# Front products of the second MoE: another order of seven products, copies by ScalarE for additions by VectorE, and another end

## The chip, the cores and the metric

The kernel runs on one core of one Trainium2 chip. TensorE multiplies, VectorE, ScalarE and GpSimd work elementwise, SyncE issues the transfers. The metric is the device time of one execution in microseconds. A matmul is fp32 split in two fp32r parts ("hi" and "lo"): three matmuls (hi x hi, hi x lo, lo x hi) add up in a PSUM bank, which only TensorE, VectorE and ScalarE can reach.

## The reference, cut to what matters

```python
x = attention(q, k, v, p)                 # 4 x 8 heads, 576 tokens, 32 packed queries
h = x @ w_in;  x = (h * cos(h)) @ w_out   # first MoE: 2304 tokens, 512 -> 2048 -> 512
p = domain_probs / (domain_probs.sum(-1, keepdims=True) + 1e-09)
for e in range(4):                        # second MoE: 512 -> 1024 -> 512 for each e
    h = np.maximum(x @ w1[e], 0.0)
    out += p[:, e:e + 1] * (h @ w2[e])
```

The change touches only the second MoE.

## The kernel before, in words

Attention and the first MoE fill the time up to about 395 us. The second MoE cuts the 2304 tokens into three thirds (h = 0, 1, 2) and w1 and w2 into eight units u of 512 hidden columns: 24 steps, n = 8h + u. Each step has a front (x @ w1) and a back (h @ w2); the back of step n stands beside the front of step n + 1.

**The front** uses a scheme with seven block products for the eight of a 2x2 block multiplication (names as in `PRODUCTS`, line 654: s1 to s4 are sums of blocks of w1, t1 to t4 of tokens). `b_pair` (line 926) makes one pair of halves, j = 0 or 1, so there are 48 pairs of seven products, each of six matmuls over 384 columns (`prod`, `mm3`). With P1 = a11 b11, P2 = a12 b21, P3 = s4 b22, P4 = a22 t4, P5 = s1 t1, P6 = s2 t2 and P7 = s3 t3: c11 = P1 + P2, u2 = P1 + P6, u3 = u2 + P7, c12 = u2 + P5 + P3, c21 = u3 - P4 (the sign lies in t4), c22 = u3 + P5. A pair holds two PSUM tiles `pa` of two banks each; there are four such tiles, and backs and fronts share them. ScalarE copies P1 into an SBUF tile `p` (line 1020); VectorE makes the five additions (line 958, three into `p`, two into a bank). Then `relu` splits each of the four blocks into hi and lo (first third; lines 1007 and 1010), or `gated` applies max(x, 0) and the token's share in one operation (line 975), and line 987 makes the sums that the back needs, lines 667 and 658 their hi and lo.

**The back** of the first third is plain (`b_back`, line 1050). For the other two thirds `b_back2` (line 1099) uses seven products again (`BACK`, line 1093), each 12 matmuls, in four tiles A to D. Each is added into one of the accumulators v, w, c11, x53, x74 by line 1132 (first time) or 1134. After the last unit of a third `final` adds x53 += v, w += x53 and x74 += v (line 1149), and `put` stores four blocks (line 1156).

**Operands.** In the first third w1 and w2 are loaded, summed, split and also stored in DRAM; in the other thirds they come back from there. The plain blocks of w2 come from a DRAM copy (`copy_w2`, line 1315, issued during the first MoE) and are split on arrival: ScalarE makes hi (`f_hi` in `split_in_place`, line 705), GpSimd or VectorE lo. Pools of this stage open at three gates; `pt`, which holds the tiles `p`, opens at gate 3 (line 1312), after the last operations of the first MoE are placed.

**The order** of all engines is made by a planner, `Plan` (line 27), and then written out as it stands (line 1375): each engine's queue is in order. It places operations one by one at the earliest time at which their inputs, buffers (`pl.slot`, with a count for each tag) and engine are free. TensorE's operations have keys (`KEYS`, by place in the step: `first`, `one`, `two`, `end` for fronts and backs, `last` for the last back); TensorE may take an operation only if its key is at most `AHEAD` = 60 above the smallest key that is left. Durations are constants of the source, times `pl.slow` in this stage. The entry `b` of `KEYS` has one key for each line of `BACK`; before, `last` has 357.6 for the fourth (w1, into x53) and 165.9 for the seventh (a22, into x74):

```python
if eng == "PE" and o["key"] > pe[0][0] + ahead:
    ok = False
...
'last': {'b': [39.4, 45.5, 37.7, 357.6, 51.2, 27.5, 165.9]},
```

Of the kernel before, what the change touches and what calls it, by code (L numbers as in the profile page):

```python
# [10 lines left out]
F32 = mybir.dt.float32  # L11
# [3 lines left out]
AF = mybir.ActivationFunctionType  # L15
ALU = mybir.AluOpType
# [10 lines left out]
class Plan:  # L27
# [35 lines left out]
    def run(self):  # L63
# [15 lines left out]
        while done < len(self.ops):  # L79
# [33 lines left out]
            t, _, o, eng = best  # L113
# [21 lines left out]
            for x, w in [(x, fin) for x in o["next"]] + [(x, t) for x in o["then"]]:  # L135
                x["wait"] -= 1
                x["at"] = max(x["at"], w)
                if not x["wait"]:
                    todo[x["eng"]].append(x)
# [7 lines left out]
def tile_packed_attention_moe_moe2(ctx: ExitStack, tc: tile.TileContext, qT, kT, vk, pT, w_in, w_out, dp, w1, w2, out, out2):  # L147
# [61 lines left out]
    def pool(name, side, bufs=1):  # L209
# [8 lines left out]
               "raw": 4, "s": 4, "aop": 8, "w2": 8, "ys": 5, "pt": -6, "g2": 13, "oacc": NTT,  # L218
# [5 lines left out]
    def dma(us, f, after=(), take=(), use=(), key=None, begun=()):  # L224
        return pl.op("SP", us, f, after, take, use, key, begun=begun)
# [700 lines left out]
    def b_pair(n, j, W, T, keys, share=None):  # L926
# [4 lines left out]
        sp = {"a": pl.slot("pa"), "c": pl.slot("pa")}  # L931
        sp["b"], sp["d"] = sp["a"], sp["c"]
        st_ = {x: pl.slot("pt") for x in ("p1", "u2", "u3")}

        def prod(i, bank, first, after):
            a, b = PRODUCTS[i]

            def f():
                if bank in "ac" and first:
                    x = psum2()  # L940
                    s[bank], s["bd"["ac".index(bank)]] = x[:, 0, :TB], x[:, 1, :TB]
# [4 lines left out]
            return pl.op("PE", 1.06, f, [W[a]["ready"], T[b]["ready"]] + after, [sp[bank]] if bank in "ac" and first else [],  # L946
                         [sp[bank], W[a]["slot"], T[b]["slot"]], keys[i])

        def tmp(name):
            s[name] = bp["pt"].tile([P, TB], F32, tag="p", name="p", bufs=6)  # L950
            return s[name]

        def add(o, x, y, after, key):
            new = o in st_ and o not in s_new
            s_new.add(o)

            def f():
                nc.vector.tensor_tensor(out=s[o] if o in s else tmp(o), in0=s[x], in1=s[y], op=ALU.add)  # L958
            return pl.op("DVE", 0.56, f, after, [st_[o]] if new else [], [sp[x], sp.get(o) or st_[o], st_[y]], key)
# [3 lines left out]
        def gated(x, half, src, after, key):  # L963
            if src in st_:
                U[x] = {"slot": st_[src]}
            else:
                U[x] = {"slot": pl.slot("s" if x == "b21" else "raw" if n == NU else "oacc")}

            def f():
                U[x]["t"] = o = s[src] if src in st_ else {  # L970
                    "b21": lambda: bp["stp"].tile([P, TB], F32, tag="s", name="u", bufs=4),
                    "raw": lambda: bp["raw"].tile([P, TB], F32, tag="raw", name="u", bufs=4),
                    "oacc": lambda: bp["oacc"].tile([P, TB], F32, tag="oacc", name="u", bufs=NTT),
                }[x if x == "b21" else "raw" if n == NU else "oacc"]()
# [3 lines left out]
            U[x]["op"] = pl.op("DVE", 0.56, f, [after, share["op"], last_out[0] if src not in st_ and x != "b21" and n == NU + 1 else None],  # L978
                               [] if src in st_ else [U[x]["slot"]],
                               [share["slot"], U[x]["slot"]] + ([sp[src]] if src in sp else []), key, port=src not in sp)  # L980
# [17 lines left out]
        def relu(f_, half, src, after, key):  # L998
# [4 lines left out]
            use = [sp[src]] if src in sp else [st_[src]]  # L1003
# [5 lines left out]
            def f_lo():  # L1009
# [4 lines left out]
            g["ready"] = pl.op("DVE", 0.56, f_lo, [h], [], [g["slot"]] + use, key, port=src not in sp)  # L1014
            return g["ready"]

        s_new = set()
# [81 lines left out]
    def b_back2(n, W, keys):  # L1099
# [4 lines left out]
        for i, (a, b, bank, new, acc, how) in enumerate(BACK):  # L1104
# [22 lines left out]
            def f_evac(ob=ob, ac=ac, acc=acc, how=how, first=first):  # L1127
                p = ob["t"][:, :, :TB]
                if first:
                    ac["t"] = (bp["ys"].tile([P, 2, TB], F32, tag="ys", name="acc", bufs=5) if acc == "x53" else  # L1130
                               bp["raw"].tile([P, 2, 512], F32, tag="raw", name="acc", bufs=4)[:, :, :TB])
                    nc.scalar.activation(ac["t"], p, AF.Copy, scale=-1.0 if how == ALU.subtract else 1.0)
                else:
                    nc.vector.tensor_tensor(out=ac["t"], in0=ac["t"] if how == ALU.subtract else p,  # L1134
                                            in1=p if how == ALU.subtract else ac["t"], op=how)

            m = pl.op("PE", 2.08, f_mm, [g["ready"] for g in gl] + [w["ready"] for w in ws] + ([] if new else [free[bank]]),
                      [ob["slot"]] if new else [], [ob["slot"]] + [g["slot"] for g in gl] + [w["slot"] for w in ws], keys[i])
            free[bank] = ac["op"] = pl.op("ACT" if first else "DVE", 0.85 if first else 0.96, f_evac, [m, ac["op"]],
                                          [ac["slot"]] if first else [], [ob["slot"], ac["slot"]], keys[i] + 8)  # L1140
            last[0] = m
        if u < NU - 1:
            return

        def final(x, y, key):
            a, b = accs[h, x], accs[h, y]

            def f():
                nc.vector.tensor_tensor(out=a["t"], in0=a["t"], in1=b["t"], op=ALU.add)

            a["op"] = pl.op("DVE", 0.95, f, [a["op"], b["op"]], [], [a["slot"], b["slot"]], key, port=True)

        def put(x, i, c, key):
            def f():
                t0 = (h - 1) * TH + c * TB
                nc.sync.dma_start(out=out2[i * 256:(i + 1) * 256, t0:t0 + TB].rearrange("(d p) n -> p d n", p=P),
                                  in_=accs[h, x]["t"])

            dma(0.4 * MB2, f, [accs[h, x]["op"]], [], [accs[h, x]["slot"]], key)
# [15 lines left out]
    def share_ops():  # L1175
# [10 lines left out]
        def f_store():  # L1186
# [11 lines left out]
            'copy': [715.7, 22.6],  # L1198
# [7 lines left out]
            'keep': [117.2, -167, 205.3, 42.6],  # L1206
            'kept': [173.4, 203.5],
            'last': {'b': [39.4, 45.5, 37.7, 357.6, 51.2, 27.5, 165.9]},
# [27 lines left out]
            'one': {'a': [7.9, 13.2, 18.6, 61.7, 42.4, 68.2, 50.5, 39, 15.5, 61.8, 75.1, 71.4, 76.6, 72.1],  # L1236
                    'b': [14.1, 54.6, 76.5, 77.4, 55.9, 66.8]},
            'out0': [-122.9, -853.4],
            'two': {'a': [-11.2, 43, 29.3, 19.8, 20.5, 46.9, 7.1, 23, 52.9, 69, 21.4, 71.4, 100.2, 84.8],
                    'b': [8, 40.1, 58.9, 16.6, 79.4, 52.2, 103.3]}}  # L1240
# [86 lines left out]
    pl.slow, pl.late = 1.04, 0.8  # L1327
# [11 lines left out]
    for n in range(NSTEP + 1):  # L1339
# [11 lines left out]
        for j in range(2):  # L1351
            b_pair(n, j, Ws[n], Ts[h], [k0 + x for x in place["a"][7 * j:7 * j + 7]], share if h else None)
# [65 lines left out]
```

## Time and profile before

| | |
|---|---|
| three timed runs | 1150.52, 1151.81, 1153.53 us; median 1151.81 |
| the profiled execution | 1149.58 us, its span 1147.8 us |
| TensorE busy | 1101.7 us (96%), 7241 matmuls |
| VectorE busy | 835.3 us (73%) |
| GpSimd busy | 633.2 us (55%) |
| ScalarE busy | 493.4 us (43%) |
| mean granted clock of TensorE | 0.987 |

PE is TensorE, PEld its loads of weights, DVE VectorE, ACT ScalarE, POOL GpSimd, SP SyncE; SPq is SyncE's sequencer, which issues transfers. L958 is line 958 of the kernel. All matmuls stand under lines 205 to 207 (`mm3`): `pa<-bop,aop` are front products, `pa<-g,w` are matmuls of the first MoE or of backs of the last two thirds, `pa<-w,g` and `pa<-at,m` others. Matmuls are pipelined and their ends are modelled. The releaser of a wait is inferred from semaphores.

### The profile page before, as it was taken

What the parts mean: (1) busy time and instruction counts of PE and PEld (TensorE: products, weight loads), DVE (VectorE), ACT (ScalarE), POOL (GpSimd) and SP (SyncE); (2) the same over time, 40 slices, a digit from 0 to 9 for tenths busy, and PEclk for the clock granted to TensorE, in tenths of its full rate; (3) what the DMA queues carried; (4) which work ended last, traced back from release to release, by engine and by line L of the source; (5) the groups of instructions that cost most, each with busy time, mean ns of one, the idle gap of its engine ahead of it and who ended that gap; (6) DMA issues with size and microseconds to landing.
All of it is one profiled execution on the core that took longest, in us unless ns stands there. A gap on an engine that the chain in (4) does not pass through costs nothing.

```text
span 1147.8 us, 19120 instructions
## 1 busy us (share of the span) xinstructions
PE 1101.7 (96%) x7241; PEld 1032.5 (90%) x7241; DVE 835.3 (73%) x1244; ACT 493.4 (43%) x852; POOL 633.2 (55%) x477
## 2 busy tenths in 40 slices
PE   6689999999999999999999999999999999999997
PEld 4568999999999988888888889999999999999997
DVE  3798777567555677787777756888887768778776
ACT  3677655445444453244334434333334343333331
POOL 1454755435422775555566546656667767645553
PEclk8699999999999999999999999999999999999999
DMA  9673436433135859787866967676667876666653
GB/s 314 231 263 118 161 116 266 188 130 141 43 105 188 280 196 325 265 301 256 291 257 263 335 259 249 232 252 233 244 227 249 306 265 238 226 227 219 228 182 110
DMA packets 96815, 257.70 MB, mean 225 GB/s; under 512 B 10892, under 2 KB 34516, under 8 KB 94548
## 3 DMA queue, kind: packets, MB, share of 16 engines
q1 hardware_dynamic: 96724, 256.48, 63.1%
q8 instruction: 57, 0.93, 0.3%
q14 instruction: 34, 0.28, 0.1%
HBM read 192.97 MB, written 71.86 MB: 231 GB/s over the span
## 4 chain that ended last, share of the span: by engine, by line
PE 78%; DVE 8%; DMA 5%; issue 4%; ACT 3%; POOL 2%; SPq 0%; POOLq 0%; ACTq 0%; DVEq 0%
PE pa L205 26%; PE pa L207 25%; PE pa L206 25%; DMA w<-w 3%; PE pa L353 2%; DVE pa L958 1%; DVE s L755 1%; POOL aop L658 1%; POOL w L658 1%; DMA kt<-kT 1%; DVE acc L1134 1%; DVE p L958 1%; DVE u L975 0%; DVE oacc L1077 0%; DVE g L1010 0%
## 5 line engine op out<-in xcount | busy, mean ns | idle before, releaser
L205 PE MATMUL pa<-g,w 128*128 128x288 f32 (+1 forms) x960 | 303.6, 316 | 2.0 <-DVE acc L1134 0.8
L206 PE MATMUL pa<-g,w 128*128 128x288 f32 (+1 forms) x960 | 301.6, 314 | 1.2 <-POOL g L590 1.2
L207 PE MATMUL pa<-g,w 128*128 128x288 f32 (+1 forms) x960 | 301.2, 314 | 0.5 <-POOL w L297 0.5
L658 POOL TENSOR_TENSOR g<-u,g 128x384 fp32r<-128x384 f32 x157 | 171.5, 1105 | 140.3 <-ACT g L667 133.5
L205 PE MATMUL pa<-bop,aop 128*128 128x384 f32 x672 | 228.8, 341 | 9.3 <-DVE p L958 4.1
L207 PE MATMUL pa<-bop,aop 128*128 128x384 f32 x672 | 226.9, 338 | 1.5 <-POOL aop L658 1.5
L206 PE MATMUL pa<-bop,aop 128*128 128x384 f32 x672 | 226.3, 337 | 1.1 <-POOL bop L658 1.1
L205 PEld LDWEIGHTS pa<-g,w 128*128 128x128 f32 x960 | 180.1, 188 | 7.9 <-issue 2.4
L206 PEld LDWEIGHTS pa<-g,w 128*128 128x128 f32 x960 | 180.2, 188 | 1.9 <-POOL g L590 1.9
L207 PEld LDWEIGHTS pa<-g,w 128*128 128x128 f32 x960 | 180.4, 188 | 1.0 <-POOL w L297 1.0
L667 ACT ACTIVATE g<-u 128x384 fp32r<-128x384 f32 x192 | 97.2, 523 | 176.8 <-DVE u L987 134.9
L590 POOL TENSOR_TENSOR g<-t,g 128x576 fp32r<-128x576 f32 x64 | 93.2, 1470 | 118.8 <-ACT g L587 117.4
L205 PEld LDWEIGHTS pa<-bop,aop 128*128 128x128 f32 x672 | 126.1, 188 | 19.1 <-DVE p L958 6.1
L206 PEld LDWEIGHTS pa<-bop,aop 128*128 128x128 f32 x672 | 126.2, 188 | 3.0 <-POOL bop L658 1.4
L207 PEld LDWEIGHTS pa<-bop,aop 128*128 128x128 f32 x672 | 126.1, 188 | 2.2 <-POOL aop L658 2.2
L958 DVE TENSOR_TENSOR p<-pa,p 128x384 f32<-128x384 f32 x144 | 79.3, 554 | 41.4 <-PE pa L207 38.7
L1134 DVE TENSOR_TENSOR acc<-pa,acc 128x768 f32<-128x768 f32 x88 | 83.9, 954 | 32.6 <-PE pa L207 31.3
L658 POOL TENSOR_TENSOR w<-w 128x512 fp32r<-128x512 f32 x62 | 86.3, 1403 | 31.4 <-ACT w L705 31.2
L205 PE MATMUL pa<-at,m 128*128 128x288 f32 x256 | 78.7, 307 | 3.1 <-DVE t L583 2.0
L206 PE MATMUL pa<-at,m 128*128 128x288 f32 x256 | 77.5, 303 | 2.8 <-POOL at L658 2.8
L205 PE MATMUL pa<-w,g 128*128 128x512 f32 x192 | 75.9, 395 | 1.9 <-DVE oacc L1077 1.9
L207 PE MATMUL pa<-at,m 128*128 128x288 f32 x256 | 77.2, 301 | 0.0
(129 smaller groups left out, 1924.8 us busy)
## 6 DMA issues: line engine op xcount, KB each, us to landing
at<-at SPq DMA_DIRECT2D x16, 1152.0 KB, 5.3
raw<-w SPq DMA_DIRECT2D x32, 512.0 KB, 5.2
w<-w SPq DMA_DIRECT2D x64, 256.0 KB, 5.0
raw<-w_in SPq DMA_DIRECT2D x6, 1024.0 KB, 6.1
raw<-w_out SPq DMA_DIRECT2D x6, 1024.0 KB, 8.0
vt<-vk SPq DMA_DIRECT2D x8, 576.0 KB, 8.5
kt<-kT SPq DMA_DIRECT2D x8, 576.0 KB, 10.5
qt<-qT SPq DMA_DIRECT2D x8, 576.0 KB, 8.6
```

What stands on the lines that cost most here:

```text
L205: nc.tensor.matmul(o, lhsT=l(0), rhs=r(0), start=first, stop=False, skip_group_check=True)
L206: nc.tensor.matmul(o, lhsT=l(0), rhs=r(1), start=False, stop=False, skip_group_check=True)
L207: nc.tensor.matmul(o, lhsT=l(1), rhs=r(0), start=False, stop=last, skip_group_check=True)
L353: nc.tensor.matmul(o(e)[32 * q:32 * q + 32, :N], lhsT=l[64 * e:64 * e + 64, 32 * q:32 * q + 32], rhs=r(q // 2, q % 2)[64 * e:64 * e + 64], ...
L590: nc.gpsimd.tensor_tensor(out=s["g"][:, 1], in0=s["t"], in1=s["g"][:, 0].bitcast(F32), op=ALU.subtract)
L658: (nc.vector if on_vector else nc.gpsimd).tensor_tensor(out=dst[:, 1], in0=src, in1=dst[:, 0].bitcast(F32), op=ALU.subtract)
L667: nc.scalar.activation(r["t"][:, 0], src(), AF.Copy)
L755: nc.vector.tensor_tensor(out=t, in0=src(a, m)(), in1=src(b, m)(), op=o)
L958: nc.vector.tensor_tensor(out=s[o] if o in s else tmp(o), in0=s[x], in1=s[y], op=ALU.add)
L1134: nc.vector.tensor_tensor(out=ac["t"], in0=ac["t"] if how == ALU.subtract else p, in1=p if how == ALU.subtract else ac["t"], op=how)
```

## The change

Within a pair the products run as P1, P2, P6, P5, P7, P3, P4 (their keys are sorted). P1, P6, P7 and P4 add up one after another in bank a, so that it holds P1, u2, u3 and c21 in turn; ScalarE copies it out after P1 (p1) and after P6 (u2). P2 stands in bank b, P5 and then P3 in bank d; ScalarE copies d after P5 (p5). VectorE adds b += p1 (c11), e = a + p5 (c22, written to a bank) and d += u2 (c12). P6 waits for the copy p1, P7 for the copy u2, P3 for the copy p5, P4 for the addition of c22. There are eight tiles `p` for six, and the gated c22 gets a tile of its own for its place.

In the last back of a third, `final` and `put` stand inside the loop: c11 is stored after i = 2; x74 += v, x53 += v and w += x53 are made, and x53 and w stored, after i = 5; the product with i = 6 is added into x74 in two halves, each stored by itself.

The planner no longer adds 0.25 us between a product and a product that follows from it, slows VectorE, ScalarE and GpSimd by 1.08 for 1.04, and has other keys for this stage and for the DRAM copies of w2.

```diff
-            for x, w in [(x, fin) for x in o["next"]] + [(x, t) for x in o["then"]]:
+            for x, w in [(x, t + us if o["fair"] and eng == "PE" == x["eng"] else fin) for x in o["next"]] + [(x, t) for x in o["then"]]:
...
-               "raw": 4, "s": 4, "aop": 8, "w2": 8, "ys": 5, "pt": -6, "g2": 13, "oacc": NTT,
+               "raw": 4, "s": 4, "aop": 8, "w2": 8, "ys": 5, "pt": -8, "g2": 13, "oacc": NTT,
...
+        def keep(x, bank, after, key):
+            return pl.op("ACT", 0.5, lambda: nc.scalar.activation(tmp(x), s[bank], AF.Copy), [after, gate[3]], [st_[x]],
+                         [sp[bank]], key)
...
-        P1 = prod(0, "a", True, [])
-        p1 = pl.op("ACT", 0.5, lambda: nc.scalar.activation(tmp("p1"), s["a"], AF.Copy), [P1, gate[3]], [st_["p1"]], [sp["a"]],
-                   k[0] + 6)
-        P6 = prod(1, "b", True, [P1])
-        u2 = add("u2", "b", "p1", [P6, p1], k[1] + 6)
-        P7 = prod(2, "c", True, [])
-        u3 = add("u3", "c", "u2", [P7, u2], k[2] + 6)
-        P5 = prod(3, "d", True, [P7])
-        c22 = add("u3", "d", "u3", [P5, u3], k[3] + 6)
-        r22 = relu(2 + j, 1, "u3", c22, k[3] + 30)
-        P2 = prod(4, "a", False, [p1])
-        relu(j, 0, "a", P2, k[4] + 8)
-        P4 = prod(5, "c", False, [u3])
-        c21 = add("c", "c", "u2", [P4], k[5] + 6)
-        relu(2 + j, 0, "c", c21, k[5] + 30)
-        P3 = prod(6, "d", False, [c22, c21])
-        c12 = add("d", "d", "u2", [P3, c21], k[6] + 6)
-        relu(j, 1, "d", c12, k[6] + 30)
+        P1 = prod(0, 0, "a", True, [])
+        p1 = keep("p1", "a", P1, k[0] + 6)
+        P2 = prod(4, 1, "b", True, [], [P1])
+        relu(j, 0, "b", add("b", "b", "p1", [P2, p1], k[1] + 6), k[1] + 30)
+        P6 = prod(1, 2, "a", False, [p1])
+        u2 = keep("u2", "a", P6, k[2] + 6)
+        P5 = prod(3, 3, "d", True, [])
+        P7 = prod(2, 4, "a", False, [u2])
+        p5 = keep("p5", "d", P5, k[3] + 6)
+        c22 = add("e", "a", "p5", [p5, P7], k[4] + 6)
+        relu(2 + j, 1, "e", c22, k[4] + 30)
+        P3 = prod(6, 5, "d", False, [p5])
+        relu(j, 1, "d", add("d", "d", "u2", [P3, u2], k[5] + 6), k[5] + 30)
+        P4 = prod(5, 6, "a", False, [c22])
+        relu(2 + j, 0, "a", P4, k[6] + 30)
...
+            if u == NU - 1 and i == 6:
+                for d in range(2):
+                    ac["op"] = pl.op("DVE", 0.56, lambda d=d, f=f_evac: f(slice(d, d + 1)), [m, ac["op"]], [],
+                                     [ob["slot"], ac["slot"]], keys[i] + 8)
+                    put(h, acc, 1, 0, keys[i] + 12, d)
+                continue
...
-        kf = keys[-1] + 20
-        put("c11", 0, 0, kf)
-        final("x53", "v", kf + 1), final("w", "x53", kf + 2), final("x74", "v", kf + 3)
-        put("x53", 0, 1, kf + 10), put("w", 1, 1, kf + 11), put("x74", 1, 0, kf + 12)
+            if u == NU - 1 and i == 2:
+                put(h, "c11", 0, 0, keys[i] + 20)
+            if u == NU - 1 and i == 5:
+                final(h, "x74", "v", keys[i] + 9), final(h, "x53", "v", keys[i] + 10)
+                put(h, "x53", 0, 1, keys[i] + 20)
+                final(h, "w", "x53", keys[i] + 11)
+                put(h, "w", 1, 1, keys[i] + 21)
...
-            'copy': [715.7, 22.6],
+            'copy': [828.4, 90],
...
-            'last': {'b': [39.4, 45.5, 37.7, 357.6, 51.2, 27.5, 165.9]},
+            'last': {'b': [23.7, 34.9, 61.9, 308.4, 80.1, 226.3, 229]},
...
-    pl.slow, pl.late = 1.04, 0.8
+    pl.slow, pl.late = 1.08, 0.8
...
-            b_pair(n, j, Ws[n], Ts[h], [k0 + x for x in place["a"][7 * j:7 * j + 7]], share if h else None)
+            b_pair(n, j, Ws[n], Ts[h], [k0 + x for x in sorted(place["a"][7 * j:7 * j + 7])], share if h else None)
```

The other entries of `KEYS` for this stage change too (`end`, `first`, `g`, `keep`, `kept`, `one`, `two`).

## Rows read from the trace of the kernel before

**Rows 1.** The page's engine line, and the view of the cores.
```profile
PE 1101.7 (96%) x7241; PEld 1032.5 (90%) x7241; DVE 835.3 (73%) x1244; ACT 493.4 (43%) x852; POOL 633.2 (55%) x477
...
core 0: 1147.8 us, clock 0.987
```

**Rows 2.** Windows: stretch, its length, busy us of each engine, clock, DMA.
```profile
395.00:692.00 297.00, 287.17 (x1436) 255.80 (x1435) 217.02 (x323) 121.52 (x233) 173.96 (x121) 1.00 0.76 274
692.00:1148.00 456.00, 443.38 (x2512) 437.34 (x2510) 355.00 (x525) 160.73 (x308) 274.53 (x235) 1.00 0.66 231
```

**Rows 3.** Waits of TensorE, whole span: waiter, releaser: us, times, longest.
```profile
PE pa L205 <- DVE p L958: 4.8, 9, 1.2
...
PE pa L205 <- DVE pa L958: 2.6, 5, 1.2
...
PE pa L205 <- DVE u L975: 2.0, 7, 0.6
PE pa L205 <- DVE oacc L1077: 1.9, 3, 1.1
PE pa L207 <- POOL aop L658: 1.5, 2, 0.8
...
PE pa L206 <- POOL bop L658: 1.1, 1, 1.1
...
PE pa L205 <- DVE acc L1134: 0.8, 1, 0.8
```

**Rows 4.** Timeline, TensorE and VectorE, 1077 to 1080: start, us, instruction.
```profile
1077.83 0.33 PE L206 MATMUL pa<-bop,aop 128*128 128x384 f32 x1
1078.01 0.34 PE L207 MATMUL pa<-bop,aop 128*128 128x384 f32 x1
1079.57 0.44 PE L205 MATMUL pa<-bop,aop 128*128 128x384 f32 x1 [1.23 <-DVE pa L958]
...
1078.97 0.55 DVE L958 TENSOR_TENSOR pa<-pa,p 128x384 f32<-128x384 f32 x1
```

**Rows 5.** Groups by line: instructions, busy us, mean ns, idle before, its releasers.
```profile
L958 DVE TENSOR_TENSOR p<-pa,p 128x384 f32<-128x384 f32 x144 | 79.3, 554 | 41.4 <-PE pa L207 38.7 <-issue 0.2
L958 DVE TENSOR_TENSOR pa<-pa,p 128x384 f32<-128x384 f32 x96 | 54.1, 564 | 30.1 <-PE pa L207 27.6 <-ACT g L1007 0.6
L975 DVE SCALAR_TENSOR_TENSOR u<-pa,share 128x384 f32<-128x384 f32 x96 | 53.0, 553 | 8.5 <-PE pa L207 6.5
L975 DVE SCALAR_TENSOR_TENSOR p<-p,share 128x384 f32<-128x384 f32 x32 | 23.7, 742 | 0.3
L1020 ACT ACTIVATE p<-pa 128x384 f32<-128x384 f32 x48 | 23.5, 491 | 45.8 <-PE pa L207 44.7 <-DMA y<-yacc 1.0
```

**Rows 6.** Timeline, ScalarE, 1075 to 1077.
```profile
1075.77 0.63 ACT L705 ACTIVATE w<-w 128x512 fp32r<-128x512 f32 x1 [3.92 <-DMA w<-w]
1076.30 0.51 ACT L667 ACTIVATE g<-u 128x384 fp32r<-128x384 f32 x1
```

**Rows 7.** Waits of ScalarE, 692 to 1148.
```profile
ACT w L705 <- DMA w<-w: 43.6, 23, 4.5
```

**Rows 8.** Timeline, TensorE, 401 to 404.
```profile
401.57 0.41 PE L205 MATMUL pa<-bop,aop 128*128 128x384 f32 x1 [0.36 <-DVE p L958]
403.12 0.44 PE L206 MATMUL pa<-bop,aop 128*128 128x384 f32 x1 [1.13 <-POOL bop L658]
```

**Rows 9.** Timeline, all engines, from 1140 to the end.
```profile
1140.40 0.96 DVE L1149 TENSOR_TENSOR acc<-acc 128x768 f32<-128x768 f32 x1
...
1141.11 0.34 PE L207 MATMUL pa<-g,w 128*128 128x384 f32 x1
1141.38 3.45 SPq L1156 DMA_DIRECT2D out<-acc  x3
1141.49 0.96 DVE L1134 TENSOR_TENSOR acc<-pa,acc 128x768 f32<-128x768 f32 x1
1142.48 1.95 DVE L1149 TENSOR_TENSOR acc<-acc 128x768 f32<-128x768 f32 x2
```

More of the change, by code (lines that the diff above doesn't have):

```diff
@@ L930, in b_pair, with prod @@
         s = {}
[L931 to L935, printed above, removed]
+        sp = {"a": pl.slot("pa"), "d": pl.slot("pa")}
+        sp["b"], sp["e"] = sp["a"], sp["d"]
+        st_ = {x: pl.slot("pt") for x in ("p1", "u2", "p5") + (("u",) if share else ())}
+        def prod(i, m, bank, first, after, begun=()):
             a, b = PRODUCTS[i]
+            opens = bank in "ad" and first
             def f():
-                if bank in "ac" and first:
+                if opens:
                     x = psum2()
-                    s[bank], s["bd"["ac".index(bank)]] = x[:, 0, :TB], x[:, 1, :TB]
+                    s[bank], s["be"["ad".index(bank)]] = x[:, 0, :TB], x[:, 1, :TB]
                 A, Bo = W[a]["t"], T[b]["t"]
@@ L944, in f @@
                     mm3(s[bank], lambda x: A[:, x, k, j * P:(j + 1) * P], lambda x: Bo[:, x, k], first and k == 0, k == 1)
-            return pl.op("PE", 1.06, f, [W[a]["ready"], T[b]["ready"]] + after, [sp[bank]] if bank in "ac" and first else [],
-                         [sp[bank], W[a]["slot"], T[b]["slot"]], keys[i])
+            return pl.op("PE", 1.06, f, [W[a]["ready"], T[b]["ready"]] + after, [sp[bank]] if opens else [],
+                         [sp[bank], W[a]["slot"], T[b]["slot"]], keys[m], begun=begun)
@@ L949, in tmp, with home @@
         def tmp(name):
-            s[name] = bp["pt"].tile([P, TB], F32, tag="p", name="p", bufs=6)
+            s[name] = bp["pt"].tile([P, TB], F32, tag="p", name="p", bufs=8)
             return s[name]
+        def home(x):
+            return sp.get(x) or st_[x]
         def add(o, x, y, after, key):
-            new = o in st_ and o not in s_new
-            s_new.add(o)
             def f():
-                nc.vector.tensor_tensor(out=s[o] if o in s else tmp(o), in0=s[x], in1=s[y], op=ALU.add)
@@ L959, in add @@
-            return pl.op("DVE", 0.56, f, after, [st_[o]] if new else [], [sp[x], sp.get(o) or st_[o], st_[y]], key)
+                nc.vector.tensor_tensor(out=s[o], in0=s[x], in1=s[y], op=ALU.add)
+            return pl.op("DVE", 0.56, f, after, [], [home(o), home(x), home(y)], key)
+        def keep(x, bank, after, key):
+            return pl.op("ACT", 0.5, lambda: nc.scalar.activation(tmp(x), s[bank], AF.Copy), [after, gate[3]], [st_[x]],
+                         [sp[bank]], key)
         U = {}
@@ L963, in gated @@
         def gated(x, half, src, after, key):
[L964 to L967, printed above, removed]
+            tag = {"b21": "s", "b22": "pt"}.get(x) or ("raw" if n == NU else "oacc")
+            U[x] = {"slot": st_["u"] if tag == "pt" else pl.slot(tag)}
             def f():
-                U[x]["t"] = o = s[src] if src in st_ else {
-                    "b21": lambda: bp["stp"].tile([P, TB], F32, tag="s", name="u", bufs=4),
+                U[x]["t"] = o = {
+                    "pt": lambda: tmp("u"),
+                    "s": lambda: bp["stp"].tile([P, TB], F32, tag="s", name="u", bufs=4),
@@ L972, in f @@
                     "raw": lambda: bp["raw"].tile([P, TB], F32, tag="raw", name="u", bufs=4),
                     "oacc": lambda: bp["oacc"].tile([P, TB], F32, tag="oacc", name="u", bufs=NTT),
-                }[x if x == "b21" else "raw" if n == NU else "oacc"]()
+                }[tag]()
                 nc.vector.scalar_tensor_tensor(out=o, in0=s[src], scalar=0.0, in1=share["t"][:, half], op0=ALU.max,
                                                op1=ALU.mult)
-            U[x]["op"] = pl.op("DVE", 0.56, f, [after, share["op"], last_out[0] if src not in st_ and x != "b21" and n == NU + 1 else None],
-                               [] if src in st_ else [U[x]["slot"]],
-                               [share["slot"], U[x]["slot"]] + ([sp[src]] if src in sp else []), key, port=src not in sp)
+            U[x]["op"] = pl.op("DVE", 0.56, f, [after, share["op"], last_out[0] if tag == "oacc" and n == NU + 1 else None],
+                               [U[x]["slot"]], [share["slot"], U[x]["slot"], sp[src]], key)
@@ L1002, in relu @@
             g = gs2[n, f_, half] = {"slot": pl.slot("g2")}
-            use = [sp[src]] if src in sp else [st_[src]]
+            use = [sp[src]]
             def f_hi():
@@ L1013, in relu @@
             h = pl.op("ACT", 0.52, f_hi, [after, gate[3]], [g["slot"]], use, key)
-            g["ready"] = pl.op("DVE", 0.56, f_lo, [h], [], [g["slot"]] + use, key, port=src not in sp)
+            g["ready"] = pl.op("DVE", 0.56, f_lo, [h], [], [g["slot"]] + use, key)
             return g["ready"]
-        s_new = set()
         k = keys
-        P1 = prod(0, "a", True, [])
-        p1 = pl.op("ACT", 0.5, lambda: nc.scalar.activation(tmp("p1"), s["a"], AF.Copy), [P1, gate[3]], [st_["p1"]], [sp["a"]],
-                   k[0] + 6)
-        P6 = prod(1, "b", True, [P1])
-        u2 = add("u2", "b", "p1", [P6, p1], k[1] + 6)
-        P7 = prod(2, "c", True, [])
-        u3 = add("u3", "c", "u2", [P7, u2], k[2] + 6)
-        P5 = prod(3, "d", True, [P7])
-        c22 = add("u3", "d", "u3", [P5, u3], k[3] + 6)
-        r22 = relu(2 + j, 1, "u3", c22, k[3] + 30)
-        P2 = prod(4, "a", False, [p1])
-        relu(j, 0, "a", P2, k[4] + 8)
-        P4 = prod(5, "c", False, [u3])
-        c21 = add("c", "c", "u2", [P4], k[5] + 6)
-        relu(2 + j, 0, "c", c21, k[5] + 30)
-        P3 = prod(6, "d", False, [c22, c21])
-        c12 = add("d", "d", "u2", [P3, c21], k[6] + 6)
-        relu(j, 1, "d", c12, k[6] + 30)
+        P1 = prod(0, 0, "a", True, [])
[13 more added lines that the diff above has]
+        relu(2 + j, 0, "a", P4, k[6] + 30)
         if share:
@@ L1125, in f_mm, with f_evac @@
                         mm3(ob["t"][:, d, :TB], l, lambda x: gl[k]["t"][:, x], new and k == 0, k == 1)
-            def f_evac(ob=ob, ac=ac, acc=acc, how=how, first=first):
-                p = ob["t"][:, :, :TB]
+            def f_evac(d=slice(0, 2), ob=ob, ac=ac, acc=acc, how=how, first=first):
+                p = ob["t"][:, d, :TB]
                 if first:
@@ L1133, in f_evac @@
                 else:
-                    nc.vector.tensor_tensor(out=ac["t"], in0=ac["t"] if how == ALU.subtract else p,
-                                            in1=p if how == ALU.subtract else ac["t"], op=how)
+                    o = ac["t"][:, d]
+                    nc.vector.tensor_tensor(out=o, in0=o if how == ALU.subtract else p, in1=p if how == ALU.subtract else o,
+                                            op=how)
             m = pl.op("PE", 2.08, f_mm, [g["ready"] for g in gl] + [w["ready"] for w in ws] + ([] if new else [free[bank]]),
@@ L1138, in b_back2 @@
                       [ob["slot"]] if new else [], [ob["slot"]] + [g["slot"] for g in gl] + [w["slot"] for w in ws], keys[i])
+            last[0] = m
+            if u == NU - 1 and i == 6:
[4 more added lines that the diff above has]
+                continue
             free[bank] = ac["op"] = pl.op("ACT" if first else "DVE", 0.85 if first else 0.96, f_evac, [m, ac["op"]],
@@ L1140, in b_back2 @@
                                           [ac["slot"]] if first else [], [ob["slot"], ac["slot"]], keys[i] + 8)
[L1141 to L1159, printed above, removed]
@@ new lines, in final, with f, put @@
+    def final(h, x, y, key):
+        a, b = accs[h, x], accs[h, y]
+        def f():
+            nc.vector.tensor_tensor(out=a["t"], in0=a["t"], in1=b["t"], op=ALU.add)
+        a["op"] = pl.op("DVE", 0.95, f, [a["op"], b["op"]], [], [a["slot"], b["slot"]], key, port=True)
+    def put(h, x, i, c, key, d=None):
+        def f():
+            t0 = (h - 1) * TH + c * TB
+            dst = out2[i * 256:(i + 1) * 256, t0:t0 + TB].rearrange("(d p) n -> p d n", p=P)
+            t = accs[h, x]["t"]
+            nc.sync.dma_start(out=dst if d is None else dst[:, d], in_=t if d is None else t[:, d])
+        dma((0.4 if d is None else 0.2) * MB, f, [accs[h, x]["op"]], [], [accs[h, x]["slot"]], key)
@@ L1197, in tile_packed_attention_moe_moe2 @@
             'blk': [206.7, 346.1, 218.8, 569.5, 339.1],
-            'copy': [715.7, 22.6],
[2 rows of a table removed]
+            'copy': [828.4, 90],
[2 rows of a table added]
             'f': [[-837.7, -739.1, -526.4, -725.8], [-47.1, 45.5, 49.7, 46.5], [-3, 19.7, 90.8, 30.6],
                   [-10.1, 23.9, 43.8, 42.1]],
[2 rows of a table removed]
[2 rows of a table added]
             'in0': [-1061.7, -368.5],
-            'keep': [117.2, -167, 205.3, 42.6],
-            'kept': [173.4, 203.5],
-            'last': {'b': [39.4, 45.5, 37.7, 357.6, 51.2, 27.5, 165.9]},
+            'keep': [62.5, -155.4, 327, 17.8],
+            'kept': [248, 256.6],
+            'last': {'b': [23.7, 34.9, 61.9, 308.4, 80.1, 226.3, 229]},
             'load': {'in': -1643.2,
@@ L1235, in tile_packed_attention_moe_moe2 @@
             'm': [-906.3, -396.8, -49.1, 19.5, -23.6],
-            'one': {'a': [7.9, 13.2, 18.6, 61.7, 42.4, 68.2, 50.5, 39, 15.5, 61.8, 75.1, 71.4, 76.6, 72.1],
-                    'b': [14.1, 54.6, 76.5, 77.4, 55.9, 66.8]},
+            'one': {'a': [30.2, 61.8, -3.7, 26.7, 37.2, 92.8, 68.1, 7.6, 56.4, 58, 64.2, 69.3, 33, 88],
+                    'b': [5.4, 38.1, 73.6, 30.4, 83.4, 54.1]},
             'out0': [-122.9, -853.4],
-            'two': {'a': [-11.2, 43, 29.3, 19.8, 20.5, 46.9, 7.1, 23, 52.9, 69, 21.4, 71.4, 100.2, 84.8],
-                    'b': [8, 40.1, 58.9, 16.6, 79.4, 52.2, 103.3]}}
+            'two': {'a': [-12.6, 6.1, 45.9, 9.2, 44.5, 52, 38.8, 28.7, 58.9, 74.7, 22.1, 72.7, 111.7, 86.3],
+                    'b': [8.5, 43.4, 61.1, 112.3, 91.7, 54.8, 96.1]}}
     def kv(n, vtag):
```

8 rows, old and new, of the table KEYS are left out of this document.

## The prediction

> **What bounds the kernel now.** I read the page's table of engines first: TensorE is busy 1101.7 of 1147.8 us, VectorE 835.3, ScalarE 493.4, and the clock stands at 0.987 of full speed [rows 1]. The change touches the second MoE alone, so I then cut the span at 395 us, where its products take over, and at 692 us, where its last sixteen steps begin (windows): TensorE is busy 287.17 of 297 and 443.38 of 456 us [rows 2]. Of the 12.6 idle us in the second stretch, the tail behind the last matmul takes 1147.8 - (1141.11 + 0.34) = 6.35 [rows 9]. So some 9.8 + 6.3 = 16.1 us are stalls between products. The matmuls themselves are the same before and after, so stalls and tail are all that can be won, and new stalls all that can be lost.
>
> The waits view says who ends them [rows 3]. Three rows belong to the chain inside a pair of blocks: VectorE's additions into p (4.8 us in 9 waits) and into a bank (2.6 in 5), and the gated blocks that free a bank (2.0 in 7): 9.4 us in 21 waits. Others are banks waiting for their evacuation (1.9 in 3 and 0.8 in 1) and operands that come late (1.5, 1.1). The view understates each: a matmul row is 0.34 us long, but its successor may start 0.17 us after it (1077.83, 1078.01), so a stop hides 0.17 us; that from 1078.01 to 1079.57 is 1.56 - 0.17 = 1.39 us against 1.23 printed [rows 4]. 21 waits hide 3.4 more: the chain costs 12.8 us, the four bank waits 2.7 + 0.7 = 3.4.
>
> **The change, part by part.** The profiled execution took 1149.58 us (span 1147.80 and 1.8 around it); the three timed runs have the median 1151.81. I sum against the first and add the difference, 2.2 us, at the end.
>
> *Work moved.* There are 48 pairs. Five additions become three: 96 of 0.555 us leave VectorE, 53 us. The block c22 is now read from a bank and not from p: its 32 gates take 0.553 for 0.742 us, 6 us less (its 16 splits in the first third also, which I leave out) [rows 5]. VectorE sheds 59 of its 572 us from 395 us on, 10%. ScalarE gets 96 copies of 0.491 us, 47 on 282. Neither engine becomes the bound (about 513 and 329 of 753 us), so none of it counts by itself; what counts is who waits.
>
> *The old chain goes.* Before, u2, u3, c22 and c21 are VectorE additions behind one another; P4 waits for u3, P3 for c22 and c21. After, of the VectorE operations in a pair only c22 holds up a product (P4). Bounds: all of the 12.8 us go, or the same waits return behind c22 and the gates, which are still on VectorE: 0. I take one such dependence in three as left: -8.5 us.
>
> *Bank waits.* They are VectorE being late with a step's evacuations; 10% less in its queue should take some of the 3.4 us, between nothing and all: -0.8.
>
> *The new chain.* P6, P7 and P3 now add into a bank that ScalarE has just copied. Such a link takes, from the start of the last matmul of the one product, 0.38 us to its reader (1141.11 to 1141.49, there VectorE) [rows 9], 0.49 for the copy [rows 5] and some 0.05 to the next matmul (1078.97 + 0.55 to 1079.57) [rows 4]: 0.92. One product of six matmuls lies between, so the next would start 7 x 0.174 = 1.22 us later anyway. The slack is 0.30 us with ScalarE free, 0.23 for c22 (0.56 for 0.49). ScalarE is busy 37% of the time, after the change 44%, mostly with operations of 0.52: half of one, 0.26, fits in the slack, so I count nothing for it, except where the queue stands. It does: the hi half of w2 (L705) waits at its head for a transfer, 43.6 us in 23 waits between 692 and 1148 us [rows 7]. At 1075.77 it had kept ScalarE idle for 3.92 us, and a conversion of g came only at 1076.30 [rows 6]. These waits take 43.6 / 456 = 9.6% of that time; it holds 32 x 3 = 96 copies, so 9 fall into one. A copy stands half a mean wait, 0.95 us, less 0.30: 0.65 x 9 = 6 us. Back products (12 matmuls, 2.1 us) make up half of a step's products, and where one is placed between, it covers that. I take half: +3. Bounds: 0 with all covered; at most 9 whole waits of 1.9 us less the slack, +14.
>
> The Trainium skill (PSUM — Partial Sum Buffer, "Engine vs sequencer instructions") speaks against this part: ScalarE's and VectorE's queues are strictly first in, first out. The trace agrees with it at the row of 1076.30; by the rule, all three links of every pair in those 16 steps hang on whatever stands ahead in that queue, the case of rival 1.
>
> *The first pair.* Ahead of 401.57 and 403.12 TensorE waits 0.36 us for an addition and 1.13 for an operand of the first tokens, 1.5 [rows 8], 1.8 with what they hide. Before, P1, P6 and P7 of both blocks could run without any copy; now P6 and P7 each wait for one, whose buffers open only when the first MoE's last operations are placed (gate 3). Two pairs side by side still give each copy a product of cover. Between -1.8 and +2.1 (two products of 1.04 us displaced): 0.
>
> *Final sums ahead of the last product.* I don't believe in this gain. PE works by key inside a window of 60: at the end a22 (i = 6, the one evacuated in halves) has key 229 and w1 (i = 3, into x53) has 308.4. So w1 is last, as now (165.9 and 357.6). Behind w1 stand its evacuation, x53 + v and w + x53, as in the rows of before: 0.96 at 1141.49, then 1.95 for two sums, the last put issued behind them [rows 9]. What the change moves forward is x74 + v, which already ran at 1140.40, beside the last matmuls. 0 us. If a22 were last after all, two half evacuations would stand in place of 2.9 us: -1.8.
>
> *The planner.* A product that follows a product is no longer planned 0.25 us late, VectorE, ScalarE and GpSimd are planned 8% slow, not 4%, and all keys of this stage are new. TensorE's order changes, its work doesn't. The copies of w2 in DRAM (keys 828 to 1458 for 716 to 874) are issued as soon as their queue is free, in the first MoE, far ahead of the step that loads them. Both count 0; what the new order itself brings is in the bounds above.
>
> Sum: -8.5 - 0.8 + 3 = -6.3; 1149.6 becomes 1143.3, and by the median of the timed runs 1151.8 becomes **1145.5**, 0.55% faster.
>
> **Rivals.**
> 1. *The wait moves to ScalarE (slower).* The copies land behind w2's conversions, and nothing covers them: +14, against -4 from the old chain (a third of 12.8, as if most of its waits too began behind such a conversion): 1151.8 + 10 = 1162. For it: in the trace the stall of 1078.01 begins just so, with g converted late behind L705, its remainder on VectorE after that, and the addition after both [rows 4, 6]. Against: back products lie between, and the conversions' places can differ. It is slower than before by what can be measured once five of the 96 copies wait a full 1.9 us less the slack (8 us) and the old chain gives back only that third. I put it at 1155 to 1162.
> 2. *Nothing to be measured.* The old waits go, and as many come from banks, operands and the copies: -8.5 + 8 = 0, 1151 give or take 3. For it: 5.3 us of the waits in [rows 3] lie outside the chain, and a tight order lets one late operand take the place of another.
> 3. *Nearly all stalls go*, with a22 last or not: -12.8 - 3.4 - 1.8 = 1134. For it: VectorE has 59 us less, and the planner allows more time. Against: the operand waits and the first pair's remain.
> That the change doesn't do what it says is part of the forecast: I hold it for the final sums.
>
> **How the numbers follow.** Forecast (1140 to 1148) 0.48, rival 3 0.12, rival 2 0.2, rival 1 0.2. What a measurement of this kernel can tell from no change is about 0.3%, 3.5 us: faster is below 1148.4, slower above 1155.3. The forecast and rival 3 are faster, 0.6; rival 2 is the same, with a little of it on either side, 0.2; rival 1 slower, 0.2. The range leaves out the far half of rivals 1 and 3: 1136 to 1157; the forecast's own is 1140 to 1148.
>
> **What would show it.** In the waits of TensorE the rows of additions (L958) shrink to a third, and a row for ScalarE's copies into p appears, with some 3 us in few waits, each beginning where an L705 stands waiting; no row for plain collisions. VectorE's busy time falls by about 60 us, ScalarE's rises by 47. The tail from the last matmul to the end stays within 0.3 us of 6.35, with x53's evacuation and two sums behind the last matmul. I am wrong if copies cost TensorE over 8 us, if the additions' waits don't fall by half, or if the tail is shorter by over 1 us.

## The result: 1163.56 us, slower where faster was forecast

The changed kernel takes 1163.56 us (median of 4 runs, 1160.87 to 1164.67) where the kernel before, run beside it, takes 1152.67 (1150.52 to 1155.21): a ratio of 1.009, 95% interval 1.0062 to 1.0118, some 11 us slower. The forecast of 1145.5 is wrong, and 1163.56 lies outside its range.

The page's engine line and the view of the cores, kernel after:

```profile
PE 1103.8 (95%) x7241; PEld 1031.5 (89%) x7241; DVE 774.7 (67%) x1138; ACT 536.5 (46%) x948; POOL 634.0 (55%) x489
...
core 0: 1158.7 us, clock 0.992
```

Against [rows 1] VectorE has lost 60.6 us and ScalarE gained 43.1; 59 and 47 were forecast. TensorE has the same 7241 matmuls and is busy 2.1 us longer, at no lower clock. So the time went where the prediction looked, into stops between products, but the other way. All waits of TensorE from 390 us on (waiter, releaser: us, times, longest), kernel after; [rows 3] are the same rows of before:

```profile
PE pa L205 <- DVE pa L959: 12.3, 18, 0.7
PE pa L207 <- DVE aop L658: 3.9, 4, 1.1
PE pa L205 <- ACT p L964: 3.0, 3, 1.4
PE pa L205 <- issue: 0.9, 1, 0.9
PE pa L205 <- ACT g L1011: 0.8, 4, 0.2
PE pa L205 <- DVE u L980: 0.8, 2, 0.4
PE pa L205 <- DVE g L1014: 0.8, 3, 0.3
PE pa L205 <- DMA w<-q7w: 0.7, 1, 0.7
```

One row decides. The three additions that are left (line 959) stop TensorE for 12.3 us in 18 waits, where the five of before did so for 4.8 + 2.6 = 7.4 in 14. Fourteen of the 18 are 0.71 to 0.73 us long: not a queue that is late now and then, but one place that is late each time. ScalarE's copies (line 964) cost 3.0 in three waits. The rows for banks not yet evacuated (oacc, acc) are gone.

To set this against the time I sum what every stop costs, hidden part included: over all pairs of neighbouring matmuls from 390 us on, the distance of their starts less the usual one (0.174 us for 384 columns). Before that is 30.1 us, after 42.6: 12.5 more, for 10.9 measured. Of the 42.6, 14.2 stand at one place: P4 of the first pair (j = 0) of a step, in the last step of the second, in 15 of the 16 steps of the later two thirds. P4 comes 0.88 or 0.89 us late in fourteen of them and 0.20 in one, and its second matmul some 0.1 later still. Timelines of one of them (start, us, instruction, idle time before and its releaser), kernel after, VectorE and then TensorE; 747.81 is the last matmul of P7, 748.87 the last of P3, 749.93 the first of P4:

```profile
746.60 0.57 DVE L959 TENSOR_TENSOR pa<-pa,p 128x384 f32<-128x384 f32 x1 [1.22 <-ACT p L964]
747.08 0.55 DVE L658 TENSOR_TENSOR g<-u,g 128x384 fp32r<-128x384 f32 x1
749.31 0.57 DVE L959 TENSOR_TENSOR pa<-pa,p 128x384 f32<-128x384 f32 x1 [1.68 <-PE pa L207]
749.91 0.56 DVE L980 SCALAR_TENSOR_TENSOR p<-pa,share 128x384 f32<-128x384 f32 x1
...
747.81 0.34 PE L207 MATMUL pa<-bop,aop 128*128 128x384 f32 x1
...
748.87 0.34 PE L207 MATMUL pa<-bop,aop 128*128 128x384 f32 x1
749.93 0.44 PE L205 MATMUL pa<-bop,aop 128*128 128x384 f32 x1 [0.73 <-DVE pa L959]
```

The addition at 749.31 is c22 = a + p5. Its inputs are P7, whose last matmul began at 747.81, and the copy p5, made before. VectorE is idle for 1.68 us ahead of it. Yet it begins 1.50 us after P7's last matmul did and 0.44 after P3's, a product that c22 doesn't contain; and P4, which c22 releases, begins 0.05 after its end. Over the 16 steps c22 stands 1.49 to 1.85 after P7 and 0.43 to 0.80 after P3. P3 is the very product that the order puts between P7 and P4 to cover c22.

### The profile page after: what moved, and what is told of

The parts are those of the page before. It is cut to its first block, busy times and chain, and to the rows that moved or that the text cites. A ratio compares the mean times of both kernels' runs of the same rounds, so it can differ in the third digit from the quotient of the medians.

```text
span 1158.7 us, 19122 instructions
## 1 busy us (share of the span) xinstructions
PE 1103.8 (95%) x7241; PEld 1031.5 (89%) x7241; DVE 774.7 (67%) x1138; ACT 536.5 (46%) x948; POOL 634.0 (55%) x489
## 4 chain that ended last, share of the span: by engine, by line
PE 85%; DVE 7%; ACT 3%; issue 2%; DMA 2%; POOL 1%; SPq 0%; DVEq 0%; ACTq 0%
PE pa L205 28%; PE pa L207 27%; PE pa L206 27%; DVE pa L959 2%; PE pa L353 2%; DMA kt<-kT 1%; DMA w<-q7w 1%; ACT p L964 1%; DMA raw<-w 1%; PE pa L1373 0%; DVE s L755 0%; SPq L197 0%; POOL at L658 0%; DVE g L1014 0%; ACT g L667 0%
## 5 line engine op out<-in xcount | busy, mean ns | idle before, releaser
L205 PE MATMUL pa<-bop,aop 128*128 128x384 f32 x672 | 230.7, 343 | 18.8 <-DVE pa L959 12.3
L658 POOL TENSOR_TENSOR g<-u,g 128x384 fp32r<-128x384 f32 x165 | 174.0, 1074 | 109.6 <-ACT g L667 101.1
L959 DVE TENSOR_TENSOR pa<-pa,p 128x384 f32<-128x384 f32 x144 | 80.9, 565 | 96.3 <-PE pa L207 55.9
L964 ACT ACTIVATE p<-pa 128x384 f32<-128x384 f32 x144 | 69.9, 488 | 141.7 <-PE pa L207 112.4
L1135 DVE TENSOR_TENSOR acc<-pa,acc 128x768 f32<-128x768 f32 (+1 forms) x90 | 84.2, 937 | 44.5 <-PE pa L207 43.7
L658 POOL TENSOR_TENSOR w<-w 128x512 fp32r<-128x512 f32 x60 | 80.0, 1340 | 56.4 <-ACT w L705 48.1
L205 PE MATMUL pa<-at,m 128*128 128x288 f32 x256 | 78.0, 305 | 3.9 <-DVE t L583 3.1
L206 PE MATMUL pa<-at,m 128*128 128x288 f32 x256 | 76.7, 299 | 2.9 <-POOL at L658 2.9
```

The lines of the kernel that those rows point to most:

```text
L205: nc.tensor.matmul(o, lhsT=l(0), rhs=r(0), start=first, stop=False, skip_group_check=True)
L206: nc.tensor.matmul(o, lhsT=l(0), rhs=r(1), start=False, stop=False, skip_group_check=True)
L658: (nc.vector if on_vector else nc.gpsimd).tensor_tensor(out=dst[:, 1], in0=src, in1=dst[:, 0].bitcast(F32), op=ALU.subtract)
L959: nc.vector.tensor_tensor(out=s[o], in0=s[x], in1=s[y], op=ALU.add)
L964: return pl.op("ACT", 0.5, lambda: nc.scalar.activation(tmp(x), s[bank], AF.Copy), [after, gate[3]], [st_[x]], [sp[bank]], key)
L1135: nc.vector.tensor_tensor(out=o, in0=o if how == ALU.subtract else p, in1=p if how == ALU.subtract else o, op=how)
```

## The theories

**N, the neighbour bank.** c22 is written to bank e, which shares a PSUM tile of two banks with d, and P3 writes d. Accesses of different engines to the two banks of one tile are kept in the program's order by a wait, though they touch different banks. P3 is written out ahead of c22, so c22 waits for P3, P4 for c22, and the cover is no cover. The planner doesn't know of this wait: in its plan P4 follows P3 without a gap.

**S, ScalarE (rival 1 of the prediction).** The copies stand behind w2's conversions in ScalarE's queue, and what follows from them is late.

**O, the order.** The new order and the planner's constants cost the time, whatever the tiles.

**M (for the last experiment).** Writing c22 to PSUM costs as such, wherever in PSUM.

In all experiments each engine keeps the changed kernel's order of work, so only the edit differs (in the second also the keys of the last back). Experiments 1 to 4 ran beside one another with the kernel before at 1152.4 us (median of 11 runs), the fifth with it at 1151.64 (13 runs).

## Experiment 1: c22 into SBUF

```diff
-            s[name] = bp["pt"].tile([P, TB], F32, tag="p", name="p", bufs=8)
+            s[name] = bp["pt"].tile([P, TB], F32, tag="p", name="p", bufs=10)
...
-                nc.vector.tensor_tensor(out=s[o], in0=s[x], in1=s[y], op=ALU.add)
+                nc.vector.tensor_tensor(out=tmp("e") if o == "e" else s[o], in0=s[x], in1=s[y], op=ALU.add)
...
-                    "pt": lambda: tmp("u"),
+                    "pt": lambda: s["e"],
```

> The changed kernel with every queue in the same order; only c22 = a + p5 is written to an SBUF tile p (ten of them for eight) and no longer to bank e, the neighbour of bank d in one PSUM tile. Theory N (neighbour bank): c22 waited for P3 besides P7, because P3 writes the other bank of the tile that c22 writes, and P4 then waited for c22, 0.88 us in 15 steps and 0.1 behind each. Then c22 starts 0.4 us after P7, P4's waits go and the time falls by 12 to 15 us, to 1148 to 1152 us, about that of the kernel before; TensorE's waits for the additions fall from 12.3 us to under 4. Theory S (ScalarE's queue, rival 1 of the prediction): the copies are late behind the conversions of w2, nothing here changes that, so 1163 give or take 2. Theory O (the new order and the planner's constants cost the time): the order is the same, 1163 give or take 2.

Measured: 1145.19 us (1142.86 to 1147.94, 6 runs), 0.9943 of before (0.9925 to 0.996). By the two ratios to before that is 1.47%, 17 us less than the changed kernel; it beats both kernels. All waits of TensorE from 390 us on, and the same place of the same step, VectorE and then TensorE (746.70 is P7's last matmul, 747.75 P3's, 747.93 P4's first):

```profile
PE pa L207 <- DVE aop L658: 3.8, 4, 1.1
PE pa L205 <- ACT p L964: 2.7, 3, 1.4
PE pa L205 <- DVE u L980: 2.0, 2, 1.6
PE pa L205 <- DVE pa L959: 1.6, 3, 0.5
PE pa L205 <- DVE g L1014: 1.6, 5, 0.4
PE pa L205 <- issue: 1.0, 1, 1.0
PE pa L205 <- DMA w<-q7w: 0.7, 1, 0.7
PE pa L206 <- POOL bop L658: 0.2, 1, 0.2
```

```profile
747.15 0.56 DVE L959 TENSOR_TENSOR p<-pa,p 128x384 f32<-128x384 f32 x1 [0.63 <-PE pa L207]
747.74 0.56 DVE L980 SCALAR_TENSOR_TENSOR p<-p,share 128x384 f32<-128x384 f32 x1
...
746.70 0.34 PE L207 MATMUL pa<-bop,aop 128*128 128x384 f32 x1
...
747.75 0.34 PE L207 MATMUL pa<-bop,aop 128*128 128x384 f32 x1
747.93 0.34 PE L205 MATMUL pa<-bop,aop 128*128 128x384 f32 x1
```

c22 now begins 0.45 us after P7, while P3 runs, and P4 follows P3 at the usual distance. The additions' waits fall from 12.3 us in 18 to 1.6 in 3. The sum over all stops falls from 42.6 to 25.9, 16.7 less, about the measured gain. That the gates of c22 take longer again (0.879 us in the mean, against 0.557 where c22 stands in a bank) costs nothing that can be seen. N holds, with a gain some 2 us above its 12 to 15. S and O had forecast no change: O falls, since the same order is now faster than the kernel before. One point is open: the edit takes away the wait and the PSUM write together, and adds two tiles p. Experiment 5 separates them.

## Experiment 2: a22 as the last product as well

```diff
-            'last': {'b': [23.7, 34.9, 61.9, 308.4, 80.1, 226.3, 229]},
+            'last': {'b': [23.7, 34.9, 61.9, 100, 80.1, 226.3, 229]},
```

This stands on top of experiment 1's edit.

> As c22_in_sbuf, and the key of w1 in the last back is 100 in place of 308.4, so that a22, evacuated in halves, is the last product and both final sums stand ahead of it. If what stands behind the last matmul sets the end, the stretch from the start of the last matmul to the end of the span falls from 6.9 us to about 5.1 (two half evacuations of 0.56 us, or one if the first runs beside the second half's matmuls, in place of 0.96 + 1.95), and the time is 1.5 to 2.5 us below c22_in_sbuf. If the last transfer sets it whatever stands ahead, nothing changes.

Measured: 1146.61 us (1144.66 to 1147.06, 6 runs), 0.9951 (0.9935 to 0.9968): nothing gained over experiment 1, a miss. Its tail, VectorE and TensorE's last matmul:

```profile
1136.64 1.83 DVE L1161 TENSOR_TENSOR acc<-acc 128x768 f32<-128x768 f32 x2
...
1137.36 0.34 PE L207 MATMUL pa<-g,w 128*128 128x384 f32 x1
1138.39 0.55 DVE L1135 TENSOR_TENSOR acc<-pa,acc 128x384 f32<-128x384 f32 x1
...
1138.85 0.95 DVE L1161 TENSOR_TENSOR acc<-acc 128x768 f32<-128x768 f32 x1
1139.72 0.55 DVE L1135 TENSOR_TENSOR acc<-pa,acc 128x384 f32<-128x384 f32 x1
```

a22's halves are evacuated at the end as meant, but v comes from the product just ahead, so all three final sums still fall beside or behind the last matmul. VectorE ends 2.91 us after the last matmul's start and not 3.32, and the span ends 6.65 after it and not 6.90: 0.25 us, below what these runs can tell.

## Experiment 3: w2's hi parts on GpSimd

```diff
-                nc.scalar.activation(r["t"][:, 0], r["t"][:, 1].bitcast(F32), AF.Copy)
+                nc.gpsimd.tensor_copy(out=r["t"][:, 0], in_=r["t"][:, 1].bitcast(F32))
```

The changed kernel otherwise; line 705's conversions leave ScalarE's queue altogether.

> The changed kernel in the same order; the hi half of w2's plain blocks (64 conversions that wait for a transfer) is made by GpSimd and not by ScalarE, so nothing on ScalarE waits for these transfers any more. Theory S: the copies p1, u2 and p5 are no longer held up behind them, the time falls by 5 to 12 us. Theories N and O: TensorE's waits for ScalarE's copies are 3.0 us in 3 waits, all ahead of 640 us, where w2 does not come from DRAM yet; the time stays within 2 us of the changed kernel, or rises by some us if GpSimd is late with w2.

Measured: 1162.03 us (1161.5 to 1162.51, 4 runs), 1.0087 (1.007 to 1.0105), against 1.009 for the changed kernel. Two of TensorE's waits in it:

```profile
PE pa L205 <- DVE pa L959: 12.3, 18, 0.7
...
PE pa L205 <- ACT p L964: 2.7, 3, 1.4
```

Nothing of the 12.3 us goes, and 2.7 of the 3.0 that copies cost stays. S is refuted: w2's conversions hold up no copy that matters.

## Experiment 4: each copy made twice

```diff
-            return pl.op("ACT", 0.5, lambda: nc.scalar.activation(tmp(x), s[bank], AF.Copy), [after, gate[3]], [st_[x]],
-                         [sp[bank]], key)
+            def f():
+                o = tmp(x)
+                for _ in range(2):
+                    nc.scalar.activation(o, s[bank], AF.Copy)
+
+            return pl.op("ACT", 0.5, f, [after, gate[3]], [st_[x]], [sp[bank]], key)
```

The changed kernel otherwise.

> The changed kernel in the same order, each of the 144 copies by ScalarE made twice into the same tile (70 us more work for ScalarE). It measures the slack of the copies' links: by the prediction 0.30 us with one product between, so a copy that is 0.49 us longer costs up to 0.2 us where nothing but one product lies between (up to half of the 144: +14 us at most), and nothing where a back product lies between. If the copies were on the path already (theory S), nearly every one would cost its 0.49: +50 us or more.

Measured: 1182.78 us (1181.71 and 1183.86), 1.0268 (1.024 to 1.0295), 19 us more than the changed kernel: above the 14 that a slack of 0.30 us allowed, far below the 50 of S. The stops, hidden parts included, are 62.3 us for 42.6, which accounts for it. P3 now stops 22 times for a copy, 6.40 us in all, and 16 of the 22 stops are 0.20 or 0.21 us long. The second copy starts 0.52 us after the first (median), so the slack of such a link is 0.52 - 0.21 = 0.31 us, as worked out; at the other six (0.34 to 0.89) the copy itself began late, 0.53 to 1.07 us after P5's last matmul did and not 0.37. That the sum is above 14 has another reason: links that stopped TensorE before pay the whole 0.52, as seven stops of P6 do. P4's stops for c22 stay as they were (12.40 in 14).

## Experiment 5: c22 in a bank of the other tile

c22 goes to bank b, beside a, and no longer to e beside d. Where c11's gate stands behind c22 in VectorE's queue c11 is overwritten unread, so c11 is lost in those pairs.

```diff
-                    s[bank], s["be"["ad".index(bank)]] = x[:, 0, :TB], x[:, 1, :TB]
+                    s[bank], s["bx"["ad".index(bank)]] = x[:, 0, :TB], x[:, 1, :TB]
+                    if bank == "a":
+                        s["e"] = s["b"]
```

> The changed kernel with one edit: c22 is still written to a PSUM bank, by the same instruction, but to bank b, the neighbour of a in the chain's own tile, after c11's gate has read b, in place of bank e beside d. Theory N (c22 waits for P3 only because P3 writes the neighbouring bank of e's tile): c22 starts 0.45 us after P7's last matmul begins, the 15 stops of P4 for c22 (12.3 us in 18 waits) fall below 3 us, and the time is 1146 give or take 3, near c22_in_sbuf's 1145.2. Rival M (what c22_in_sbuf won comes from c22 not being written to PSUM at all, for instance from a cheaper write or from a bank freed earlier): the stops stay above 8 us and the time is 1163 give or take 2. Of its own, P4, which writes bank a, must now stand behind whatever reads b; c22 itself reads a, so P4 hangs on it in any case, and c11's gate was done long before: no new wait is expected from it under either theory, at most 1 us.

Measured: 1153.08 us (1150.77 to 1156.31, 10 runs), 1.0018 (1.0004 to 1.0031): 0.7% below the changed kernel, and between the two expectations. Two waits of TensorE, and the place in question, VectorE and then TensorE (748.07 is P3's last matmul, 748.68 P4's first):

```profile
PE pa L205 <- DVE p L982: 4.4, 14, 0.7
...
PE pa L205 <- DVE pa L961: 1.6, 3, 0.5
```

```profile
747.47 0.57 DVE L961 TENSOR_TENSOR pa<-pa,p 128x384 f32<-128x384 f32 x1 [0.64 <-PE pa L207]
748.07 0.56 DVE L982 SCALAR_TENSOR_TENSOR p<-pa,share 128x384 f32<-128x384 f32 x1
...
748.07 0.34 PE L207 MATMUL pa<-bop,aop 128*128 128x384 f32 x1
748.68 0.44 PE L205 MATMUL pa<-bop,aop 128*128 128x384 f32 x1 [0.27 <-DVE p L982]
```

c22, by the same instruction into PSUM as in the changed kernel, begins 0.45 us after P7 (in the median of the 16 steps too) and ahead of P3's end. The additions' waits are back at 1.6 in 3. M falls: the tile decides, not the PSUM write, and not the tiles p either, of which there are eight here. The time is 8 us above experiment 1 because of a wait that I had put at nothing, and it is N again. c22's gate (line 982) now reads b, P4 writes a, the neighbour, and P4 waits for the gate: 748.07 + 0.56 = 748.63, P4 at 748.68. P4 stops so 16 times, 0.45 us in the mean (0.23 to 0.82), hidden part included, 7.2 us; the sums over all stops, 33.1 and 25.9, differ by the same 7.2. One mechanism thus shows at two places, a VectorE write held by a matmul and a matmul held by a VectorE read. That it is a wait of the program, not of the memory, is read from the trace, which names by semaphores who releases each; d and e in tiles of one bank each were not tried.

## Why the prediction was wrong, point by point

**The old chain goes: the step that failed.** It says that "of the VectorE operations in a pair only c22 holds up a product (P4)" and leaves a third of the waits. That is so by the data. I asked what c22 holds up, and only by its data what holds up c22. The dependence left costs 14.2 us, more than the whole old chain at 12.8, and the additions' waits rose from 7.4 us printed to 12.3 instead of falling to a third. With the neighbour out of the way at this place (experiment 1) they are 1.6, and the time is 1145.19 for the 1145.5 forecast. That this is so close is luck in part: by the stops of the profiled executions experiment 1 gains 30.1 - 25.9 = 4.2 us on the kernel before, and the terms below miss in both directions.

The material lay open. In the diff, P3 names c21 among its predecessors in the kernel before, though c12 = u2 + P5 + P3 has no c21 in it: c21 is written to c, and P3 adds into d, its neighbour. And the stop in [rows 4], from which I took the hidden part of a stop, is this very wait: the matmul at 1079.57 is P3 into d, released by an addition into c. I read it as arithmetic. Set against the program's order of products, most of what I called the old chain was the same mechanism: in 17 of its 21 waits in [rows 3], 7.9 of the 9.4 us, the releaser works in the other bank of the product's tile. P3 (bank d) stands 12 times behind the addition into c or the gate that reads c, P5 (d) four times behind u3's reading of c, P2 (a) once behind u2's reading of b. Only three are what I had named, P4 behind u3 and P3 behind c22. This is read from the releasers; no run set the tiles of the kernel before apart.

The Trainium skill (PSUM — Partial Sum Buffer, "PSUM bank collisions raise a hardware error") asks for guards by bank and 32-partition quadrant, since each bank is a memory of its own. By that rule P3 in d and c22 in e need no guard, which is how I read the diff. The waits here are coarser: in the median c22 begins 0.44 us after the start of P3's last matmul when it is in e, and 0.61 ahead of it when it is in b. The measurement decides for this kernel's program: guards go by the two-bank tile.

**The new chain, +3.** The size came out, 3.0 us in three waits, but by luck: the cause was another. None of the three stands behind line 705. They come at 397.59, 493.75 and 528.75, in the first third, and the first belongs to the first pair, below. ScalarE and then TensorE at the last of them, kernel after:

```profile
527.69 0.63 ACT L667 ACTIVATE aop<-raw 128x512 fp32r<-128x512 f32 x1 [1.53 <-DMA raw<-w]
528.23 0.85 ACT L964 ACTIVATE p<-pa 128x384 f32<-128x384 f32 x2
...
528.75 0.44 PE L205 MATMUL pa<-bop,aop 128*128 128x384 f32 x1 [1.23 <-ACT p L964]
```

The copy stands behind an operand's conversion that waits for its transfer: the queue was the right fear, at the wrong line. But the matmuls at 493.75 and 528.75 are the first of P2, which adds to no copied bank. P2 writes b, and the copy that releases it (of u2, from 528.23 on) reads a, the other bank of its tile: the neighbour again. The three waits for additions that experiment 1 leaves (1.6 us) are of this kind too: P6, which writes a, behind c11's addition into b. The slack of the copies' links, 0.30, holds (0.31 in experiment 4). That for c22, 0.23 worked out, is 0.17 in experiment 1: c22 ends at 747.71, P4 comes at 747.93, 0.05 of that for the link.

**Bank waits, -0.8.** The 1.9 + 0.8 us in [rows 3] went entirely, more than I took. But operands that come late rose from 1.5 + 1.1 to 3.9 in 4, and now by a split that stands on VectorE: even, as rival 2 said of such waits.

**The first pair, 0.** Right: 1.37 us in one wait (397.59) for the 1.5 of [rows 8].

**Final sums, 0.** Right. w1 is last, and its evacuation and two sums stand behind the last matmul as in [rows 9]; kernel after:

```profile
1151.78 0.34 PE L207 MATMUL pa<-g,w 128*128 128x384 f32 x1
1152.15 0.96 DVE L1135 TENSOR_TENSOR acc<-pa,acc 128x768 f32<-128x768 f32 x1 [1.06 <-PE pa L207]
1153.14 1.95 DVE L1161 TENSOR_TENSOR acc<-acc 128x768 f32<-128x768 f32 x2
```

The tail is 1158.7 - 1152.12 = 6.58 us against 6.35. The 1.8 that I gave a22 as last product was too much: experiment 2 found 0.25, with the final sums still at the end.

**Rival 1** named 1155 to 1162, near the time, but by an engine that experiment 3 clears. **The planner** at 0 hid the point: its new order is sound for the dependences that it is told, and the one that it isn't told stands at its tightest place. Planning anew with this dependence stated was not tried.

## What to carry over

Where two engines work side by side in PSUM, ask of each operation what touches the other bank of its tile, too: a product placed as cover is none if its bank lies beside the one that the covered operation writes or reads. A short stop that comes back at the same place in every step points to a dependence, not to a late queue: take the idle engine's next instruction and see which matmul its start follows at the usual distance of such a link (0.44 us after P3 here; after P7, whose result it reads, 1.50). Before such a chain is planned anew, one operand put into SBUF tells what the tile costs.

## What the runs showed that I had not expected

- A wait on the neighbouring bank of a tile, in both directions between TensorE and VectorE: 0.9 us a time when a product of six matmuls stands in it, 0.45 in the mean with a gate of 0.56. ScalarE's reading of a bank holds a matmul into its neighbour in the same way (P2 at 528.75).
- From the start of a product's last matmul to the VectorE operation it releases: 0.44 or 0.45 us in these chains, where I had taken 0.38 from an evacuation of 768 columns [rows 9]; to ScalarE's copy it is 0.37 in the median. From a VectorE operation's end to the matmul: 0.05.
